# A GeGLU feed-forward kernel: the first transfers put on one queue without a gate, the first tokens turned per block of 128

## The chip, the cores and the metric

The kernel runs on one core of a Trainium2 chip. The metric is the time of one execution on the device in microseconds (us). The profile is that of one execution, taken by the hardware profiler; its times are counted from the first instruction.

## The reference

```python
B, S, D, F = 32, 32, 1024, 3584
x: (B, S, D); w_gate, w_up: (D, F); w_down: (F, D)      # all bfloat16
def reference(x, w_gate, w_up, w_down):
    return (_gelu(x @ w_gate) * (x @ w_up)) @ w_down     # gelu, tanh form
```

There are 1024 tokens. Matrix products of 1024 x 1024 x 3584 (twice) and 1024 x 3584 x 1024 are computed.

## The kernel before

**Tiling.** TensorE contracts over 128 partitions. The 1024 input features are 8 steps `dk` of 128 (feature p*8+dk sits on partition p), the 3584 hidden features are 28 chunks `m` of 128. For each chunk and each stretch of tokens the kernel accumulates a gate product ("G") and an up product ("U") in PSUM over the 8 steps, ScalarE takes the gelu of the gate into a buffer `tb`, and VectorE multiplies it by the up product into `hT`. When all of `hT` is there, the second phase multiplies it by `w_down` (line 418) and writes the result out.

**Parts.** A part is one chunk with one stretch of tokens. The first 8 chunks are done in three stretches: tokens 0 to 255 (parts 0 to 7, called XA), tokens 256 to 511 (parts 8 to 15, XB, itself of two halves XB1 and XB2 of 128 tokens), tokens 512 to 1023 (XC2). All other chunks have two stretches of 512. Parts 0 to 15 keep gate and up side by side in one PSUM bank (bank m), so that part 8 can begin only when VectorE has multiplied part 0 out of the same bank.

**x has to be turned.** Features must lie on partitions (`xT`). For XA, two blocks of 128 tokens are loaded (`xa`, line 292). TensorE turns dk 0 to 4 of them by matmuls with an identity (`turn_xa`, lines 344 to 355), ScalarE copies the result from PSUM to `xT` (line 432; the banks and steps are in `XA_PS`, line 131), and VectorE turns dk 5 to 7 (line 455). The rest of x is loaded in 512-byte rows into `xs`, which lies in a part of `hT` that is still free (line 283), and VectorE turns it (line 470).

**First weights.** The first 8 chunks need 1024 columns of both weight matrices. They are loaded step by step, wg and wu of dk 0, of dk 1 and so on, 256 KB each (`load_w0`, line 288). The text calls them wg0 to wg7 and wu0 to wu7. The later weights come in 1 MB groups (line 277), the first of which waits until XC2 has landed (`gate_w`, lines 303 to 309).

**Order of the work.** Every engine's program is written out by hand. `steps` (lines 156 to 183) is TensorE's order: turn XA; dk 0 of parts 0 to 7; dk 1 to 5 of all eight together; dk 6 and 7 of the parts 0 to 3, then of 4 to 7; then parts 8 to 11, in dk 0 to 3 first for XB1 and then for XB2; then the rest part by part. `dve_order` (lines 186 to 194) is VectorE's: "E" is the multiplication of a part, A, B, C and D are transposes of XB1, XB2, XC2 and all of XB at one dk. SyncE issues the first block of `xa`, all sixteen first weights, and then, behind a wait until wu5 has landed (line 299), one half of every x piece. ScalarE issues the second block of `xa` and, behind the same wait, the other half of every x piece. Before its first real matmul TensorE runs ten matmuls on constants (`WARM`, line 390).

The lines that decide which transfer is issued when:

```python
            ctx.set(("xa", side), ew.do(lambda: eng.dma_start(
                xa[:, side, :], xa_r[:, side, :]), clock=Q_XA[side]))
            yield
            if side == 0:
                for k in range(DK):
                    for w in ("wg", "wu"):
                        load_w0(ew, eng, w, k)
            ew.wait(Q_W0[("wu", 5)], ctx.get(("wu0", 5)))
            for q in XPIECES:
                load_x(ew, eng, q, side)
```

Of the kernel before, what the change touches and what calls it, by code (L numbers as in the profile page):

```python
# [5 lines left out]
P = 128  # L6
BF16 = mybir.dt.bfloat16
FP32 = mybir.dt.float32
ACTF = mybir.ActivationFunctionType
# [75 lines left out]
def bass_standalone__geglu_ffn__sampling_kernel(  # L85
# [13 lines left out]
    DK = D // P  # L99
# [82 lines left out]
    one_by_one(range(8, 12), 6)  # L182
# [3 lines left out]
    dve_order = []  # L186
    mix = ("E0 E1 E2 A0 E3 A1 A2 A3 B0 B1 B2 B3 E4 D4 D5 E5 D6 D7 E6 E7 "
           "C0 E8 C1 E9 C2 E10 E11 C3 C4 E12 C5 E13 C6 C7 E14 E15")
    for w in mix.split():
        if w[0] == "E":  # L190
            dve_order.append(("E", int(w[1:])))
        else:
            dve_order.append(("T", int(w[1:])) + {"A": XB1, "B": XB2, "C": XC2, "D": XB}[w[0]])
    dve_order += [("E", p) for p in range(NSHORT, NPART)]
# [25 lines left out]
    Q_X = {(q, s): _Clock(f"x{i}{s}", 16) for i, q in enumerate(XPIECES) for s in range(2)}  # L220
    Q_W0 = {(w, k): _Clock(f"{w}0k{k}", 16) for k in range(DK) for w in ("wg", "wu")}
    Q_WG = [_Clock(f"wg{j}", 16) for j in range(NG)]
# [9 lines left out]
    with ExitStack() as es:  # L232
# [54 lines left out]
        def load_w0(ew, eng, w, k):  # L287
            ctx.set((w + "0", k), ew.do(lambda: eng.dma_start(  # L288
                big[w][:, k, :], w_r[w][:, k, 0:NBIG * P]), clock=Q_W0[(w, k)]))
# [12 lines left out]

# [22 lines left out]
        def prog_sp(eng):  # L325
            sp = _Eng(ctx, eng, None)
            for _ in early_loads(sp, eng, 0):
                pass
            wd_mine = [k for k in range(len(wd_groups)) if k % 2 == 0]
# [14 lines left out]
        def turn_xa(pe, eng, b, dk):  # L344
            pe.wait(Q_XA[b], ctx.get(("xa", b)))
            j = next(j for j, (_, k0, k1) in enumerate(XA_PS) if k0 <= dk < k1)
            bank, k0, k1 = XA_PS[j]
            o = 256 * (dk - k0) + P * b
            last = dk == k1 - 1 and b == 1
            v = pe.do(lambda: eng.matmul(  # L350
                ps[:, bank, o:o + P],
                xa[:, b, :].rearrange("p (j k) -> p j k", k=DK)[:, :, dk],
                ident[:, :], start=(dk == k0 and b == 0), stop=last), mark=last)
            if last:
                ctx.set(("XP", j), v)

        def part_step(pe, eng, opened, i, key, dk, tok):
# [6 lines left out]
            if j is None:  # L364
                pe.wait(Q_W0[(w, dk)], ctx.get((w + "0", dk)))
# [4 lines left out]
            for jx, (xbank, k0, k1) in enumerate(XA_PS):  # L370
                if t0 == XA[0] and (xbank == bank or k0 <= dk < k1):
                    pe.wait(C_ACT, ctx.get(("XA", jx)))
            if t0 == XA[0] and dk >= XA_DVE[0]:
                pe.wait(C_DVE, ctx.get("XD"))
# [14 lines left out]

        WARM = [512] * 6 + [128] * 4  # L390

# [34 lines left out]
        def prog_act(eng):  # L426
            act = _Eng(ctx, eng, C_ACT)
            act.do(lambda: eng.activation(warm[:, 0:1], const0, ACTF.Gelu_apprx_tanh))
            for _ in early_loads(act, eng, 1):
                for j, (bank, k0, k1) in enumerate(XA_PS):  # L430
                    act.wait(C_PE, ctx.get(("XP", j)))
                    ctx.set(("XA", j), act.do(lambda: eng.activation(  # L432
                        xT[:, k0:k1, XA[0]:XA[1]],
                        ps[:, bank, 0:256 * (k1 - k0)].rearrange("p (k t) -> p k t", t=256), ACTF.Copy)))
            for i, (m, t0, t1, (gb, g0, g1), us) in enumerate(parts):
# [101 lines left out]
```

## Time and profile before

| what | value |
|---|---|
| median of 3 runs | 299.68 us (299.42 to 299.73) |
| profiled execution, span from first to last instruction | 298.2 us |
| the same execution's time in all | not listed beside its span |
| first phase, matmuls of line 381 on the chain | 61% of the span |
| second phase, matmuls of line 418 on the chain | 32% of the span |
| mean granted clock of TensorE | 1.000 |
| bytes moved | 26.43 MB, mean 89 GB/s |

The span leaves out what lies before the first and after the last instruction, so it is shorter than the run times. "PE" is TensorE's matmuls, "PEld" its weight loads, DVE is VectorE, ACT ScalarE, POOL GpSimd, SP SyncE; "PEq" or "SPq" is the queue of an engine that issues. The chain of waits follows the work that ended last back from the last instruction; the page gives each engine's share of it. A table of stretches gives each engine's busy time in it, with the number of instructions in brackets, the granted clock, the busy share of the DMA engines and the bytes they moved. Matmuls are pipelined: their durations overlap (a 128x256 matmul is shown with 272 ns, but eight of them start within 0.87 us), so a pace is read from starts.

### The profile page before, as it was taken

Reading aid. Unit: us, or ns where it says so; the run is one execution under the profiler, and the core shown is the slowest. Engines: PE = TensorE matmul, PEld = TensorE weight load, DVE = VectorE, ACT = ScalarE, POOL = GpSimd, SP = SyncE. Lnnn points to the kernel's source line nnn. Section 1 sums busy time; section 2 is a strip of 40 time slices with the busy share of each in tenths; the row PEclk is TensorE's granted clock in tenths of the full one; section 3 lists DMA queues with packets and bytes.
Section 4 is the critical chain, followed back from the end, with each engine's and each line's share of the span. In section 5 each row is a group of like instructions: output and inputs, shape, how many; then the busy total and the mean of one; then the engine's idle time right before and its main releaser. Section 6 shows DMA issues by size and latency. Waiting matters only on the chain.

```text
span 298.2 us, 3515 instructions
## 1 busy us (share of the span) xinstructions
PE 294.9 (99%) x1552; PEld 149.1 (50%) x1552; DVE 64.3 (22%) x108; ACT 42.2 (14%) x78; POOL 7.9 (3%) x14
## 2 busy tenths in 40 slices
PE   8999999999999999999999999999999999999997
PEld 5889644444444444444444444444444444444446
DVE  4669721111122111122111122110000000000000
ACT  3032211121111121111112111110000000000000
POOL 1001001020000002001000000000000000000000
DMA  7988004856009301943103000000000100010001
GB/s 258 391 197 263 22 2 133 289 186 240 0 0 294 131 0 31 372 162 92 51 0 141 0 2 0 0 0 20 18 18 20 35 18 18 20 35 18 18 20 35
DMA packets 17807, 26.43 MB, mean 89 GB/s; under 512 B 1025, under 2 KB 11393, under 8 KB 17793
## 3 DMA queue, kind: packets, MB, share of 16 engines
q1 hardware_dynamic: 13840, 16.78, 17.2%
q0 software_dynamic: 2176, 8.39, 7.9%
q10 hardware_dynamic: 1776, 1.05, 1.3%
q8 instruction: 12, 0.20, 0.3%
q14 instruction: 3, 0.02, 0.0%
HBM read 24.12 MB, written 2.10 MB: 88 GB/s over the span
## 4 chain that ended last, share of the span: by engine, by line
PE 94%; DMA 3%; SPq 2%; issue 0%; ACT 0%
PE ps L381 61%; PE ps L418 32%; DMA wubig<-in_w_up_dram 3%; SPq L288 2%; SPq L292 0%; ACT xT L445 0%
## 5 line engine op out<-in xcount | busy, mean ns | idle before, releaser
L418 PE MATMUL ps<-wd,hT 128*128 128x512 bf16 (+1 forms) x476 | 96.9, 366 | 0.0
L381 PE MATMUL ps<-xT,wubig 128*128 128x512 bf16 (+2 forms) x400 | 79.8, 336 | 0.3 <-DMA wubig<-in_w_up_dram 0.3
L381 PE MATMUL ps<-xT,wgbig 128*128 128x512 bf16 (+2 forms) x400 | 79.8, 336 | 0.2 <-ACT xT L432 0.2
L418 PEld LDWEIGHTS ps<-wd,hT 128*128 128x128 bf16 x476 | 46.6, 98 | 50.4
L479 DVE TENSOR_TENSOR hT<-tb,ps 128x512 bf16<-128x512 f32 (+1 forms) x64 | 39.0, 616 | 136.6 <-PE ps L381 136.6
L439 ACT ACTIVATE tb<-ps 128x512 f32<-128x512 f32 (+1 forms) x64 | 34.2, 544 | 158.4 <-PE ps L381 156.9
L381 PEld LDWEIGHTS ps<-xT,wubig 128*128 128x128 bf16 x400 | 38.1, 98 | 32.1 <-DMA wubig<-in_w_up_dram 0.7
L381 PEld LDWEIGHTS ps<-xT,wgbig 128*128 128x128 bf16 x400 | 38.0, 98 | 31.6 <-DMA wgbig<-in_w_gate_dram 0.3
L381 PE MATMUL ps<-xT,wgsmall 128*128 128x512 bf16 x128 | 30.2, 379 | 0.0
L381 PE MATMUL ps<-xT,wusmall 128*128 128x512 bf16 x128 | 30.2, 379 | 0.0
L485 DVE CAST xT<-ps 128x512 bf16<-128x512 f32 (+1 forms) x8 | 5.3, 658 | 88.1 <-PE ps L418 88.1
L381 PEld LDWEIGHTS ps<-xT,wusmall 128*128 128x128 bf16 x128 | 12.5, 98 | 15.1
L381 PEld LDWEIGHTS ps<-xT,wgsmall 128*128 128x128 bf16 x128 | 12.5, 98 | 15.1
L445 ACT ACTIVATE xT<-ps 128x512 bf16<-128x512 f32 (+1 forms) x9 | 5.2, 573 | 93.1 <-PE ps L418 93.1
L470 DVE STREAM_TRANSPOSE xT<-hT 128x128 bf16<-128x128 bf16 (+2 forms) x20 | 13.4, 714 | 0.0
L455 DVE STREAM_TRANSPOSE xT<-hT 32x192 bf16<-32x192 bf16 x16 | 8.3, 516 | 4.6 <-DMA hT<-in_x_dram 4.1
L277 POOL DMA_DIRECT2D wubig<-in_w_up_dram x3 | 2.7, 886 | 63.3 <-PE ps L381 63.3
L395 PE MATMUL ps<-const-bfloat16-1.0 128*128 128x512 bf16 (+1 forms) x10 | 3.1, 498 | 0.8 <-PEq L522 0.8
L277 POOL DMA_DIRECT2D wusmall<-in_w_up_dram x2 | 2.0, 992 | 47.3 <-PE ps L381 26.0
L271 POOL DMA_DIRECT2D wd<-in_w_down_dram x3 | 2.3, 764 | 19.1 <-PE ps L381 19.1
L395 PEld LDWEIGHTS ps<-const-bfloat16-1.0 128*128 128x128 bf16 x10 | 1.2, 139 | 2.4 <-issue 2.4
L432 ACT ACTIVATE xT<-ps 128x512 bf16<-128x512 f32 (+1 forms) x3 | 1.4, 526 | 2.2 <-PE ps L350 2.2
(10 smaller groups left out, 4.5 us busy)
## 6 DMA issues: line engine op xcount, KB each, us to landing
wd<-in_w_down_dram SPq DMA_DIRECT2D x4, 1024.0 KB, 11.5
wgbig<-in_w_gate_dram SPq DMA_DIRECT2D x3, 1024.0 KB, 5.6
wubig<-in_w_up_dram POOLq DMA_DIRECT2D x3, 1024.0 KB, 9.7
wd<-in_w_down_dram POOLq DMA_DIRECT2D x3, 1024.0 KB, 11.4
wgbig<-in_w_gate_dram SPq DMA_DIRECT2D x8, 256.0 KB, 5.5
wubig<-in_w_up_dram SPq DMA_DIRECT2D x8, 256.0 KB, 5.6
wgsmall<-in_w_gate_dram SPq DMA_DIRECT2D x2, 1024.0 KB, 5.8
wusmall<-in_w_up_dram POOLq DMA_DIRECT2D x2, 1024.0 KB, 9.7
```

The costliest lines, as they stand in the source:

```text
L271: ew.do(lambda: eng.dma_start(wd[:, a:b, :], wd_r[:, a:b, :]), clock=clock)
L277: ctx.set((w, j), ew.do(lambda: eng.dma_start(wbuf(w, buf)[:, :, 0:gsz * P], w_r[w][:, :, c0 * P:(c0 + gsz) * P]), clock=q))
L288: ctx.set((w + "0", k), ew.do(lambda: eng.dma_start(big[w][:, k, :], w_r[w][:, k, 0:NBIG * P]), clock=Q_W0[(w, k)]))
L381: v = pe.do(lambda: eng.matmul(ps[:, bank, f0:f1], wbuf(w, buf)[:, dk, slot * P:(slot + 1) * P], xT[:, dk, t0:t1], start=first, stop=last ...
L395: pe.do(lambda: eng.matmul(ps[:, 0, 0:n], ones_w, ones_x[:, 0:n], start=True, stop=True), mark=False)
L418: v = pe.do(lambda: eng.matmul(ps[:, b, 0:ncols], hT[:, m, tc * P:(tc + 1) * P], wd[:, m, col0:col0 + ncols], start=(m == 0), stop=(m == F ...
L439: ctx.set(("A", i), act.do(lambda: eng.activation(t_bufs[i % NTB][:, 0:t1 - t0], ps[:, gb, g0:g1], ACTF.Gelu_apprx_tanh)))
L445: ctx.set(("E", ji), act.do(lambda: eng.activation(osb[:, tc, col0:col0 + ncols], ps[:, b, 0:ncols], ACTF.Copy)))
L455: v = dve.do(lambda: eng.transpose(xT[32 * a:32 * (a + 1), XA_DVE[0]:XA_DVE[1], XA[0]:XA[1]].rearrange("p k (b t) -> p k b t", t=P)[:, :, ...
L470: v = dve.do(lambda: eng.transpose(xT[:, dk, q[0]:q[1]].rearrange("p (c i) -> p c i", i=32), src))
L479: ctx.set(("D", i), dve.do(lambda: eng.tensor_tensor(hT[:, m, t0:t1], t_bufs[i % NTB][:, 0:t1 - t0], ps[:, ub, u0:u1], ALU.mult)))
L485: ctx.set(("E", ji), dve.do(lambda: eng.tensor_copy(osb[:, tc, col0:col0 + ncols], ps[:, b, 0:ncols])))
```

## The change

1. SyncE issues all early transfers, and none of them waits for anything: both blocks of `xa`, the sixteen first weights, XB1 behind wu5, XB2 behind wu6 and XC2 behind wu7. ScalarE issues no transfer any more. The four quarters of an x piece go out in the order 0, 2, 1, 3.
2. The weights of dk 0 and dk 1 are loaded in halves of 512 columns (chunks 0 to 3 and 4 to 7), each with a semaphore of its own.
3. dk 0 of XA is copied from PSUM in two copies, one per block of 128 tokens (banks 7 and 6), dk 1 and 2 in one (bank 5), dk 3 and 4 in one (bank 4). TensorE does dk 0 of the gate for chunks 0, 1, 2, 3 and 7 first for block 0, then for block 1; the other products of dk 0 come in a new order.
4. Parts 8 to 11 are done with 256 tokens at once in dk 0 to 5, and VectorE turns XB only in pieces of 256 tokens (D0 to D7), D0 and D1 ahead of the first multiplication.
5. The warm-up has one matmul of 128 columns in place of four.

```diff
+    XAFTER = [(("wu", 5), (256, 384)), (("wu", 6), (384, 512)), (("wu", 7), (512, 1024))]
...
-    XA_PS = [(3, 0, 1), (4, 1, 3), (5, 3, 5)]
+    XA_PS = [(7, 0, 1, 0, 1), (6, 0, 1, 1, 2), (5, 1, 3, 0, 2), (4, 3, 5, 0, 2)]
     XA_DVE = (5, 8)
+    W0_HALVED = 2
+    w0_pieces = [(w, k, c) for k in range(8) for w in ("wg", "wu")
+                 for c in ((0, 4), (4, 8))[:2 if k < W0_HALVED else 1]]
+    w0_pieces = [(w, k, c if k < W0_HALVED else (0, NBIG)) for w, k, c in w0_pieces]
...
-    for key, ps_ in (("G", (0, 1, 2, 3, 7, 6, 4)), ("U", (0, 1, 2, 3)), ("G", (5,)), ("U", (7, 6, 4, 5))):
+    for b in range(2):
+        steps += [(p, "G", 0, (P * b, P * (b + 1))) for p in (0, 1, 2, 3, 7)]
+    for key, ps_ in (("G", (6,)), ("U", (0, 1, 2, 3)), ("G", (5,)), ("U", (7, 6, 5)), ("G", (4,)), ("U", (4,))):
         steps += [(p, key, 0, None) for p in ps_]
...
-    together(range(8, 12), 0, 4, XB1)
-    together(range(8, 12), 0, 4, XB2)
-    together(range(8, 12), 4, 6)
+    together(range(8, 12), 0, 6)
...
-    mix = ("E0 E1 E2 A0 E3 A1 A2 A3 B0 B1 B2 B3 E4 D4 D5 E5 D6 D7 E6 E7 "
+    mix = ("D0 D1 E0 E1 D2 E2 E3 D3 E4 D4 E5 D5 E6 D6 D7 E7 "
            "C0 E8 C1 E9 C2 E10 E11 C3 C4 E12 C5 E13 C6 C7 E14 E15")
...
         def load_x(ew, eng, q, side):
             c0, c1 = q[0] // 32, q[1] // 32
-            for a in (2 * side, 2 * side + 1):
+            for a in (side, 2 + side):
...
-        def early_loads(ew, eng, side):
-            ctx.set(("xa", side), ew.do(lambda: eng.dma_start(
-                xa[:, side, :], xa_r[:, side, :]), clock=Q_XA[side]))
-            yield
-            if side == 0:
-                for k in range(DK):
-                    for w in ("wg", "wu"):
-                        load_w0(ew, eng, w, k)
-            ew.wait(Q_W0[("wu", 5)], ctx.get(("wu0", 5)))
-            for q in XPIECES:
-                load_x(ew, eng, q, side)
+        def load_w0(ew, eng, pc):
+            w, k, (c0, c1) = pc
+            ctx.set(("w0", pc), ew.do(lambda: eng.dma_start(
+                big[w][:, k, c0 * P:c1 * P], w_r[w][:, k, c0 * P:c1 * P]), clock=Q_W0[pc]))
+
+        def early_loads(ew, eng):
+            for b in range(2):
+                ctx.set(("xa", b), ew.do(lambda: eng.dma_start(
+                    xa[:, b, :], xa_r[:, b, :]), clock=Q_XA[b]))
+            for pc in w0_pieces:
+                load_w0(ew, eng, pc)
+                for after, q in XAFTER:
+                    if after == pc[:2]:
+                        for side in range(2):
+                            load_x(ew, eng, q, side)
...
-        WARM = [512] * 6 + [128] * 4
+        WARM = [512] * 6 + [128]
```

More of the change, by code (lines that the diff above doesn't have):

```diff
@@ L192, in bass_standalone__geglu_ffn__sampling_kernel @@
         else:
-            dve_order.append(("T", int(w[1:])) + {"A": XB1, "B": XB2, "C": XC2, "D": XB}[w[0]])
+            dve_order.append(("T", int(w[1:])) + {"C": XC2, "D": XB}[w[0]])
     dve_order += [("E", p) for p in range(NSHORT, NPART)]
@@ L220, in bass_standalone__geglu_ffn__sampling_kernel @@
     Q_X = {(q, s): _Clock(f"x{i}{s}", 16) for i, q in enumerate(XPIECES) for s in range(2)}
-    Q_W0 = {(w, k): _Clock(f"{w}0k{k}", 16) for k in range(DK) for w in ("wg", "wu")}
+    Q_W0 = {pc: _Clock(f"{pc[0]}0k{pc[1]}c{pc[2][0]}", 16) for pc in w0_pieces}
     Q_WG = [_Clock(f"wg{j}", 16) for j in range(NG)]
@@ L285, in load_x @@
             ctx.set(("x", q, side), v)
-        def load_w0(ew, eng, w, k):
-            ctx.set((w + "0", k), ew.do(lambda: eng.dma_start(
-                big[w][:, k, :], w_r[w][:, k, 0:NBIG * P]), clock=Q_W0[(w, k)]))
-        def early_loads(ew, eng, side):
-            ctx.set(("xa", side), ew.do(lambda: eng.dma_start(
-                xa[:, side, :], xa_r[:, side, :]), clock=Q_XA[side]))
-            yield
-            if side == 0:
-                for k in range(DK):
-                    for w in ("wg", "wu"):
-                        load_w0(ew, eng, w, k)
-            ew.wait(Q_W0[("wu", 5)], ctx.get(("wu0", 5)))
-            for q in XPIECES:
-                load_x(ew, eng, q, side)
+        def load_w0(ew, eng, pc):
[12 more added lines that the diff above has]
+                            load_x(ew, eng, q, side)
         def gate_w(ew, j):
@@ L326, in prog_sp @@
             sp = _Eng(ctx, eng, None)
-            for _ in early_loads(sp, eng, 0):
-                pass
+            early_loads(sp, eng)
             wd_mine = [k for k in range(len(wd_groups)) if k % 2 == 0]
@@ L345, in turn_xa @@
             pe.wait(Q_XA[b], ctx.get(("xa", b)))
[L346 to L349, printed above, removed]
+            j, (bank, k0, k1, b0, b1) = next(
+                (j, c) for j, c in enumerate(XA_PS) if c[1] <= dk < c[2] and c[3] <= b < c[4])
+            o = P * ((b1 - b0) * (dk - k0) + b - b0)
+            last = dk == k1 - 1 and b == b1 - 1
             v = pe.do(lambda: eng.matmul(
@@ L352, in turn_xa @@
                 xa[:, b, :].rearrange("p (j k) -> p j k", k=DK)[:, :, dk],
-                ident[:, :], start=(dk == k0 and b == 0), stop=last), mark=last)
+                ident[:, :], start=(dk == k0 and b == b0), stop=last), mark=last)
             if last:
@@ L364, in part_step @@
             if j is None:
-                pe.wait(Q_W0[(w, dk)], ctx.get((w + "0", dk)))
+                pc = next(q for q in w0_pieces if q[:2] == (w, dk) and q[2][0] <= m < q[2][1])
+                pe.wait(Q_W0[pc], ctx.get(("w0", pc)))
             else:
@@ L369, in part_step @@
                 pe.wait(C_DVE, ctx.get(("D", bank_before[i][bank])))
-            for jx, (xbank, k0, k1) in enumerate(XA_PS):
-                if t0 == XA[0] and (xbank == bank or k0 <= dk < k1):
+            for jx, (xbank, k0, k1, b0, b1) in enumerate(XA_PS):
+                if t1 <= XA[1] and (xbank == bank or (k0 <= dk < k1 and t0 < P * b1 and P * b0 < t1)):
                     pe.wait(C_ACT, ctx.get(("XA", jx)))
-            if t0 == XA[0] and dk >= XA_DVE[0]:
+            if t1 <= XA[1] and dk >= XA_DVE[0]:
                 pe.wait(C_DVE, ctx.get("XD"))
@@ L428, in prog_act @@
             act.do(lambda: eng.activation(warm[:, 0:1], const0, ACTF.Gelu_apprx_tanh))
[L429 to L434, printed above, removed]
+            for j, (bank, k0, k1, b0, b1) in enumerate(XA_PS):
+                act.wait(C_PE, ctx.get(("XP", j)))
+                nt = P * (b1 - b0)
+                ctx.set(("XA", j), act.do(lambda: eng.activation(
+                    xT[:, k0:k1, P * b0:P * b1],
+                    ps[:, bank, 0:nt * (k1 - k0)].rearrange("p (k t) -> p k t", t=nt), ACTF.Copy)))
             for i, (m, t0, t1, (gb, g0, g1), us) in enumerate(parts):
```

## The prediction

> **What bounds the kernel now.** I read the page first: engines' shares, slices, chain.
>
> ```profile
> span 298.2 us, 3515 instructions
> PE 294.9 (99%) x1552; PEld 149.1 (50%) x1552; DVE 64.3 (22%) x108; ACT 42.2 (14%) x78; POOL 7.9 (3%) x14
> ...
> PE   8999999999999999999999999999999999999997
> PE 94%; DMA 3%; SPq 2%; issue 0%; ACT 0%
> ```
>
> TensorE is the bound; the only things on the chain that are not its own work lie at the start. So I read the chain of waits in order of time:
>
> ```profile
> 8.17 0.44 SPq L288
> 8.61 0.04 issue
> 8.66 8.20 DMA wubig<-in_w_up_dram
> 16.86 0.05 issue
> 16.91 182.50 PE ps L381 x951
> 199.40 96.78 PE ps L418 x476
> ```
>
> From 16.91 us on TensorE runs to the end without a stop (182.50 + 96.78 us). The last thing that held it was one transfer: the up-weights' row 7 (wu7), the last of the sixteen first pieces, issued at 8.66, landed at 16.86. The end of the kernel is "when does wu7 land" plus fixed matmul work, unless the change makes another wait later. Next, the stretches around it (columns: busy us of PE, PEld, DVE, ACT, POOL, granted clock, DMA share, GB/s):
>
> ```profile
> 4.50:5.50 1.00, 0.80 (x10) 0.63 (x9) 0.94 (x3) 1.00 (x3) 0.00 (x0) 1.00 1.03 272
> 5.50:14.00 8.50, 8.50 (x80) 7.46 (x78) 6.93 (x14) 0.26 (x1) 0.00 (x0) 1.00 1.05 392
> 14.50:16.50 2.00, 2.00 (x20) 1.66 (x18) 0.00 (x0) 0.00 (x0) 0.00 (x0) 1.00 1.09 258
> 16.50:17.50 1.00, 0.74 (x8) 0.54 (x7) 0.00 (x0) 0.28 (x1) 0.00 (x0) 1.00 0.64 145
> 17.50:19.50 2.00, 2.00 (x22) 1.80 (x20) 1.86 (x6) 1.47 (x6) 0.00 (x0) 1.00 1.06 305
> ```
>
> From 5.5 to 14 us the DMA engines are full and move weights at 392 GB/s. When the x pieces (512-byte rows) flow, the engines are just as full but move 258 to 305. Last, the queues between 14.0 and 15.6 us:
>
> ```profile
> q1 hardware_dynamic: 466, 0.36, 76.7%
> q10 hardware_dynamic: 272, 0.13, 31.6%
> q8 instruction: 1, 0.02, 4.1%
> ```
>
> q1 is SyncE's queue, q10 ScalarE's, and q8 one fetch of 16 KB of instructions (it starts at 14.45 and takes 1.05 us on one of the 16 engines). In the trace's semaphore updates fifteen engines had delivered their part of wu7 by 15.57; the sixteenth came at 16.86. The piece before it, wg7, landed at 14.76 (issued at 8.17, 6.6 us to landing).
>
> **The change, part by part.** All is measured against the span of 298.2; the page gives that execution no other time, and the median of the runs, 299.68, lies 1.48 us above it, which I add unchanged.
>
> *x pieces ahead of the last weights.* Before, x waits until wu5 is in (12.74) and then goes out on two queues beside wg6 to wu7. After, SyncE issues 4 pieces of XB1 (64 KB each) behind wu5 and 4 of XB2 behind wu6. wu7 thus has 2 x 262 KB ahead of it in its own queue. Without any x, wu7 would have landed one weight piece after wg7: wu5 to wg7 is three pieces in 14.76 - 12.73 = 2.03 us, 0.68 each, so 15.44. XB1 and XB2 at 258 GB/s take 1.02 us each, 2.03 together: 17.47. The trace has no 512-byte rows on one queue alone, so I bound it: as fast as weights (392 GB/s) 1.34 together; at the slowest full us with x in flight (145 GB/s) 3.62. I take 258, the nearest row: the same pieces at the same place. The Trainium skill, "DMA: Bandwidth & Descriptors", section "Issuing engines are not separate DMA queues", says that all queues end on the same 16 engines, so that a second queue saves only issue time; by it one queue is as fast as two and 2.03 stands, while if half the pace were lost with the second queue it would be 4.06.
>
> *Issue time.* Before, SyncE issued 16 weights from 0.73 to 8.66: (8.66 - 0.73) / 16 = 0.496 us each with gaps. After, wu7 has 29 issues ahead of it: 2 xa, 8 halves, 8 whole pieces (dk 2 to 5), 4 of XB1, wg6, wu6, 4 of XB2, wg7. 0.73 + 29 x 0.496 = 15.1 us; at 0.47 a piece, 14.4. The shortest 256 KB landing in the trace is 2.9 us after issue (xa's first block, 0.73 to 3.63), which gives 17.3 to 18.0. So the issue side reaches about the same time as the bytes; they do not add up, the later one counts. wg7 and wu7 are what stands behind the x issues on SyncE; nothing else of the first 35 us but XC2 and the small weights does.
>
> *The late engine.* The fetch belongs to TensorE's own instructions and comes at nearly the same place (3 warm-up matmuls fewer, 5 more in dk 0). It should again meet the queue before wu7 and hold one engine up. Bounds: 0 us (a gap in the queue lets that engine catch up, which an issue-bound queue gives) and 16.86 - 15.57 = 1.29 us. Between them I take 0.6: wu7 lands at 17.47 + 0.6 = 18.1.
>
> *Chunk 0 by blocks, halves, warm-up.* Three cold 128-column warm-up matmuls go (0.107 each, 0.32 us). The first copy needs only block 0, is 128 columns wide (the 128x256 copy took 0.384), and xa's second block now follows the first instead of sharing with it. Ten 128-column matmuls at 0.056 replace five at 0.109: nothing. Waits added on TensorE are for halves: behind each stands the whole matmul order. A half is issued every 0.496 us, the eight take 4.0 instead of 2.0 us, and wu1's second half leaves at about 0.73 + 9 x 0.496 = 5.2, 2.6 us later than wu1 before. With 2.0 us to landing (an estimate: 2.9 for the first 256 KB less half of its bytes' time and the ramp) it lands near 7.2, where wu1 landed before at 7.16; TensorE wants it at 7.8. I expect the first real matmul near 4.7 (before 4.93) and dk 0 done about 0.2 us earlier (between 0.0 and 0.7). TensorE would then want wu7 at 16.38 - 0.2 = 16.2. All of this lies under the wait until 18.1 and is worth nothing; were the cover gone, it would be those 0.2 us.
>
> *Transposes and parts 8 to 11.* 64 matmuls of 128 columns (19.43 to 23.00, 3.57 us) become 32 of 256 (0.1093 each, 3.50): -0.07. Eight transposes of 128x128 and four of 128x256 become eight of 128x256, 0.585 us each; D0 and D1 need XB2, which lands before wg7, and are done while TensorE waits. In TensorE's terms (part 8 starts 2.5 us after wu7) the fourth product E3 then ends about 0.08 us before it is wanted, so a stall there is 0 to 0.1; I take 0. XC2 follows wu7 and is in by about 22.5; its transposes begin near 25.5. Cover for all of them: the products E4 to E7 are wanted only 7 us after part 8's start. ScalarE loses six x issues (12.75 to 16.5), which ended before its first gelu at 17.23: nothing.
>
> Sum: TensorE resumes at 18.1 + 0.05 = 18.15 instead of 16.91, +1.24; -0.07; span 298.2 + 1.17 = 299.4, time 300.85, so **300.9 us**.
>
> **The rivals.**
> *Hidden (within 0.2%).* The queue never stops, x runs at 305 GB/s (0.86 each: 17.16) and the late engine catches up: TensorE resumes at 17.2, +0.3 - 0.07: 299.9. For it: the DMA share of 1.09 at 258 GB/s is already not the best x pace. Against: an instruction fetch in the same stretch.
> *Faster.* The gated start and two competing queues were the trouble, and one ungated queue removes it: x at 392 GB/s gives 15.44 + 1.34 = 16.78, the hole at 4.5 to 5.5 (272 instead of 392 GB/s, 0.31 us) is filled, 16.5, and without a late engine (its usual lag is 14.76 - 14.58 = 0.18) 16.3. Then TensorE's own pace counts: 16.91 less its stall of 0.43 and 0.2 of earlier start, 16.28: -0.63 - 0.07, 299.0. It decides if wu7 lands before 16.3. Against: 0.52 MB more ahead of wu7.
> *One queue is slow for x.* At 145 GB/s wu7 lands 1.59 later: 302.4. For it: the row 16.50:17.50; against: that stretch has a share of 0.64, so it lacked issues, not pace.
> *The clock falls.* The wait of 16.2 to 18.1 would send TensorE back to the pace of its first 3.4 us (128 columns in 0.107 instead of 0.056 until 4.18); 3.4 us at half rate cost 1.7: 302.6. Against: the stall of 0.43 us at 16.4 changed no matmul's time. The same loss at the start (fewer warm-up matmuls, then 0.3 us idle before xa lands) would be covered: 16.2 + 1.7 = 17.9, before 18.1. The Trainium skill, "TensorE: Matmul & The Clock Gate", section "Part 1: The HAM clock gate", asks for an idle window of about 3.4 us before the clock drops; by it a wait of 1.9 us leaves it alone, and this rival falls away.
>
> **How the numbers follow.** Forecast (300.3 to 301.6) 0.50, hidden 0.21, faster 0.10, slow queue 0.11, clock 0.08. A measurement of this kernel tells 0.2% (0.6 us) from no change: faster is below 299.1, slower above 300.3. Slower 0.50 + 0.11 + 0.08 = 0.69, less 0.01 for its lower edge: 0.68; same 0.22; faster 0.10. The range leaves the quickest tenth and part of the clock rival out: 299.4 to 302.2.
>
> **What would show it.** TensorE's longest early wait should be for wu7 (or wg7), ending near 18.1, with a rise of the start-to-resume time of 1.2 us and 279 us of matmuls behind it as before; the x pieces must have landed before wg7. The issue times on SyncE must reach 14.4 to 15.1 for wu7. If fifteen engines deliver wu7 by 17.5 and one later, the late engine is shown. I am wrong if wu7 lands before 16.3, if TensorE's waits after 20 us exceed 0.2 us, or if 256-column matmuls take longer than 0.11 us apiece after the wait.

## The result, and the profile after

| | before | after |
|---|---|---|
| median of 5 runs each | 299.68 us (299.42 to 299.84) | 307.69 us (306.03 to 308.58) |
| profiled execution, span | 298.2 us | 304.7 us |
| the same execution's time | | 306.03 us |
| mean granted clock of TensorE | 1.000 | 0.994 (two of the five runs 0.989) |

The ratio is 1.0257, with a 95% interval of 1.0230 to 1.0284: the change makes the kernel slower by 8.0 us, where 1.2 were forecast. A run more than 1.5% above the fastest of its kernel counts as slow and is left out of the ratio, which happened once below. The profiled execution is the fastest of the five; the median run took 1.66 us more at the same mean clock, and no trace shows where. The page of the kernel after, cut to the rows shown before:

```profile
span 304.7 us, 3455 instructions
PE 298.0 (98%) x1522; PEld 149.1 (49%) x1522; DVE 64.2 (21%) x104; ACT 42.6 (14%) x79; POOL 7.9 (3%) x14
...
PEclk9998999999999999999999999999999999999999
```

TensorE still is the bound, and the row of the granted clock has a dent in its fourth slice (22.9 to 30.5 us) that a glance passes over. The end of the chain of waits, in order of time:

```profile
14.65 0.43 SPq L294
15.08 0.04 issue
15.12 6.66 DMA wubig<-in_w_up_dram
21.78 0.05 issue
```

The same transfer holds TensorE as before, wu7, but it lands at 21.78 us instead of 16.86. TensorE resumes at 21.83 and then needs 304.7 - 21.83 = 282.87 us to the end, where it needed 298.2 - 16.91 = 281.29 before. So of the 6.5 us that the span grew by, 4.92 lie before the resume and 1.58 behind it. The stretches (busy us of PE, PEld, DVE, ACT, POOL; granted clock, DMA share, GB/s) show both parts:

```profile
5.50:14.00 8.50, 8.02 (x73) 6.35 (x73) 6.97 (x14) 0.30 (x1) 0.00 (x0) 1.00 0.94 319
14.50:16.50 2.00, 2.00 (x21) 1.79 (x20) 0.00 (x0) 0.00 (x0) 0.00 (x0) 1.00 1.10 278
16.50:17.50 1.00, 0.72 (x8) 0.41 (x6) 0.00 (x0) 0.00 (x0) 0.00 (x0) 1.00 1.22 287
17.50:19.50 2.00, 0.97 (x8) 0.39 (x5) 0.00 (x0) 0.00 (x0) 0.00 (x0) 1.00 1.06 286
19.50:22.00 2.50, 0.45 (x3) 0.26 (x4) 1.14 (x2) 0.00 (x0) 0.00 (x0) 1.00 1.22 210
22.40:25.80 3.40, 3.40 (x19) 2.42 (x17) 2.70 (x7) 1.61 (x6) 0.00 (x0) 0.50 0.67 125
```

From 5.5 to 14 us, where almost nothing but weights flows, the DMA engines deliver 319 GB/s instead of 392, and TensorE starts 73 matmuls instead of 80. From 16.5 to 22 it starves: 19 matmuls in 5.5 us. From 22.4 to 25.8 it is busy all the time at half its clock. The matmuls themselves, in the timeline of TensorE (start, duration, line, tiles, shape, count):

```profile
20.33 0.28 PE L386 MATMUL ps<-xT,wgbig 128*128 128x256 bf16 x1 [1.25 <-DMA wgbig<-in_w_gate_dram]
21.83 0.28 PE L386 MATMUL ps<-xT,wubig 128*128 128x256 bf16 x1 [1.22 <-DMA wubig<-in_w_up_dram]
...
23.62 1.06 PE L386 MATMUL ps<-xT,wubig 128*128 128x256 bf16 x4
...
26.02 0.60 PE L386 MATMUL ps<-xT,wgbig 128*128 128x256 bf16 x4
```

Four matmuls of 256 columns take 1.06 us at 23.6 and 0.60 at 26.0. The trace's clock records put the half rate at 22.42 to 25.83, 3.41 us, which costs half of that, 1.71.

When the pieces landed, by the semaphore updates of the trace (us). A piece has landed when the last of the 16 DMA engines has delivered its share; the mean over the 16 is beside it, since one engine alone can be more than 1 us behind:

| | wg0 | wu1 | wg2 | wu5, mean / last | XB1 | wg6 | XB2 | wg7 | wu7, mean / last | stage wu5 to wu7 by the means |
|---|---|---|---|---|---|---|---|---|---|---|
| before | 4.76 | 7.16 | 7.98 | 12.39 / 12.73 | | 13.40 | | 14.76 | 15.32 / 16.86 | 2.93 |
| after | 5.72 | 8.75 | 9.47 | 14.59 / 15.55 | 16.56 | 17.20 | 19.57 | 20.28 | 20.27 / 21.78 | 5.69 |

This splits the 4.92 us: 2.20 had already been lost when wu5 was in, before the first piece of x was due; the stage from wu5 to wu7, the only one in which x lies ahead of weights, became 2.76 longer; the last engine is as far behind the mean of wu7 as before (1.51 and 1.54). Three questions go to the chip: what makes wu5 late, what makes x cost 2.8 us, and what makes the clock fall.

### The profile page after: what moved, and what is told of

It is laid out like the page before. It is cut to its first block, busy times and chain, and to the rows that moved or that the text cites. A ratio compares the mean times of both kernels' runs of the same rounds, so it can differ in the third digit from the quotient of the medians.

```text
span 304.7 us, 3455 instructions
## 1 busy us (share of the span) xinstructions
PE 298.0 (98%) x1522; PEld 149.1 (49%) x1522; DVE 64.2 (21%) x104; ACT 42.6 (14%) x79; POOL 7.9 (3%) x14
## 4 chain that ended last, share of the span: by engine, by line
PE 92%; SPq 4%; DMA 2%; issue 0%; ACT 0%
PE ps L386 60%; PE ps L423 32%; SPq L294 3%; DMA wubig<-in_w_up_dram 2%; SPq L288 1%; SPq L299 0%; ACT xT L450 0%
## 5 line engine op out<-in xcount | busy, mean ns | idle before, releaser
L386 PE MATMUL ps<-xT,wgbig 128*128 128x512 bf16 (+2 forms) x389 | 80.9, 345 | 1.9 <-DMA wgbig<-in_w_gate_dram 1.8
L386 PE MATMUL ps<-xT,wubig 128*128 128x512 bf16 (+1 forms) x384 | 80.7, 347 | 1.9 <-DMA wubig<-in_w_up_dram 1.8
L386 PEld LDWEIGHTS ps<-xT,wusmall 128*128 128x128 bf16 x128 | 12.5, 98 | 15.1
L386 PEld LDWEIGHTS ps<-xT,wgsmall 128*128 128x128 bf16 x128 | 12.5, 98 | 15.1
L450 ACT ACTIVATE xT<-ps 128x512 bf16<-128x512 f32 (+1 forms) x9 | 5.2, 573 | 93.1 <-PE ps L423 93.1
L475 DVE STREAM_TRANSPOSE xT<-hT 128x256 bf16<-128x256 bf16 (+1 forms) x16 | 13.4, 857 | 6.8 <-DMA hT<-in_x_dram 6.8
L437 ACT ACTIVATE xT<-ps 128x128 bf16<-128x128 f32 (+1 forms) x4 | 1.6, 436 | 2.0 <-PE ps L354 2.0
```

Of the source, the lines that this page charges most:

```text
L386: v = pe.do(lambda: eng.matmul(ps[:, bank, f0:f1], wbuf(w, buf)[:, dk, slot * P:(slot + 1) * P], xT[:, dk, t0:t1], start=first, stop=last ...
L450: ctx.set(("E", ji), act.do(lambda: eng.activation(osb[:, tc, col0:col0 + ncols], ps[:, b, 0:ncols], ACTF.Copy)))
L475: v = dve.do(lambda: eng.transpose(xT[:, dk, q[0]:q[1]].rearrange("p (c i) -> p c i", i=32), src))
```

## Experiments

Each ratio is against the kernel before, timed beside it (its medians lie between 299.56 and 299.74 us). Landings are those of the profiled execution, wu5 and wu7 by the mean over the 16 engines unless the last is named; the stage is the time between these means. Expectations that give a landing or the length of a stage mean the last engine's.

### What makes wu5 late

**One part undone.** In the kernel after, the first weights in whole pieces:

```diff
-    W0_HALVED = 2
+    W0_HALVED = 0
```

> The changed kernel with the weights of dk 0 and 1 in whole pieces again (18 issues of 256 KB instead of 26); x still goes ahead of wg6 and wg7. In the changed kernel wu5 landed at 15.55 us (before: 12.73), 2.8 us late before any x had moved. Theory A (the halves starve the DMA engines: one issue each 0.47 us carries 128 KB): wu5 lands near 13.0, wu7 near 19.2 (the x stage keeps its 6.2 us from wu5 to wu7), TensorE resumes there, about 2.6 us sooner than in the changed kernel: 303.5 to 305.5 us, depending on whether the clock still falls (1.7 us). Theory B (the single ungated queue itself is slow, halves or not): wu5 stays near 15.5, the time stays at 306 to 308.6.

305.24 us (303.39 to 307.87), 1.0196 [1.0131, 1.0261]. wu5 landed at 13.35 instead of 14.59: better, but not back at 12.39. So the halves are not all of it. The trace shows the clock at half rate from 7.20 to 10.62.

**x behind all weights.** In the kernel after:

```diff
-    XAFTER = [(("wu", 5), (256, 384)), (("wu", 6), (384, 512)), (("wu", 7), (512, 1024))]
+    XAFTER = [(("wu", 7), (256, 384)), (("wu", 7), (384, 512)), (("wu", 7), (512, 1024))]
```

> The changed kernel with all x pieces issued behind wu7; the halves stay. Theory A (x ahead costs what its bytes cost, halves cost 2.8 us before it): wu5 lands near 15.5 as in the changed kernel, wu7 2.8 us later at 18.3 instead of 21.8; the clock holds, since the waits of TensorE are shorter. XB2 then lands near 20.5 and D0, D1, which VectorE does ahead of the first product, end near 21.7, so that part 8 waits about 1 us: 301 to 303 us. Theory B (the order of x does not matter, the queue is slow anyway): above 305 us.

305.15 us (304.3 to 305.61), 1.0184 [1.0162, 1.0205]: a miss. wu5 landed at 14.41, as late as in the kernel after, so x behind it is not what delays it; wu7 at 17.45, a stage of 3.04 as before the change. The gain was lost again elsewhere, as the timeline of TensorE shows (waits in brackets):

```profile
22.88 0.61 PE L386 MATMUL ps<-xT,wgbig 128*128 128x256 bf16 x2 [1.28 <-DVE hT L484]
24.05 0.72 PE L386 MATMUL ps<-xT,wgbig 128*128 128x256 bf16 x2 [0.56 <-DVE hT L484]
```

XB2 now landed at 21.26. The transposes D0 and D1 stand ahead of the first multiplications in VectorE's order, and part 8 cannot have its bank before the product E0: TensorE waits 1.28 and 0.56 us for VectorE, and the clock falls (half rate 23.87 to 27.28).

**Both together.**

> Both edits: whole pieces and x behind wu7, still one queue without a gate, everything else of the change as it is. If the two causes are independent and make up the loss: wu7 lands at 15.3 to 16.0 and TensorE has no wait over 0.5 us before 17 us; D0 and D1 are late (XB2 lands near 17.8, E0 follows at 19.2 where part 8 wants it at 18.7), 0.3 to 1 us: 299.0 to 300.5 us. If something else of the change costs (copies by block, warm-up, order of transposes), 301 us or more.

303.40 us (302.95 to 303.56), 1.0126 [1.0111, 1.0141], again above what was expected. wu5 13.17, wu7 16.11. The waits of TensorE's weight loads between 4 and 24 us (total, times, longest):

```profile
PEld ps L386 <- DMA wgbig<-in_w_gate_dram: 1.9, 1, 1.9
PEld ps L386 <- DVE hT L484: 1.5, 4, 0.8
```

The first weights landed at 6.59 instead of 4.76, although they went out in whole pieces with no x in sight. What is left of the change in these microseconds is the second block of `xa` on SyncE's queue.

**The halves alone**, put into the kernel before:

```diff
-                for k in range(DK):
-                    for w in ("wg", "wu"):
-                        load_w0(ew, eng, w, k)
+                for pc in w0_pieces:
+                    load_w0(ew, eng, pc)
```

> The kernel before with nothing but the weights of dk 0 and 1 in halves (x gated on two queues as before). If halves starve the engines: wu5 lands at about 15.0 to 15.5, x follows it by the gate, wu7 lands about 2 us later than before, near 18.5 to 19: 301.5 to 302.5 us. If the halves alone cost nothing and the slow first 11 us belong to the second block of xa on the same queue or to the x issues, 299.5 to 300 us.

300.69 us (300.55 to 301.31), 1.0045 [1.0031, 1.0060]. The stretch that had 392 GB/s and 80 matmuls before:

```profile
5.50:14.00 8.50, 7.47 (x68) 6.38 (x67) 6.97 (x14) 0.42 (x1) 0.00 (x0) 1.00 0.92 306
```

306 GB/s and 68 matmuls. wg2 landed at 10.01 (before 7.98), wu5 at 14.13, 1.74 later than before. TensorE waited 1.2 us for wg2, and then, from 10.05, ran to the end without a stop: wu7's last engine came at 17.91, but TensorE, late already, was no longer ahead of it. The halves do not lie under the wait for wu7: they move wu7 (by 1.65 us in the mean), and here they also made TensorE wait earlier.

**The second block of `xa` on SyncE alone**, put into the kernel before:

```diff
-            ctx.set(("xa", side), ew.do(lambda: eng.dma_start(
-                xa[:, side, :], xa_r[:, side, :]), clock=Q_XA[side]))
+            for b in range(2 if side == 0 else 0):
+                ctx.set(("xa", b), ew.do(lambda: eng.dma_start(
+                    xa[:, b, :], xa_r[:, b, :]), clock=Q_XA[b]))
```

> The kernel before with the second block of xa issued by SyncE behind the first instead of by ScalarE; nothing else. In the two runs with whole pieces on one queue, wg0 landed at 6.27 and 6.59 us (before: 4.76), and TensorE stood still for 2.0 us in its cold first stretch. Theory Q (the second block in front of the weights on the same queue is what makes wg0 late): wg0 lands after 5.5, TensorE's first real matmuls wait, the clock rises a window late: 300.5 to 302.5 us. Rival (the lateness has to do with what follows on the queue, or with the other edits): wg0 lands at 4.8 to 5.3 and the time is 299.4 to 300.2 us.

300.52 us (10 runs, 299.82 to 301.7), 1.0030 [1.0012, 1.0047]. The profiled execution is one of the three at 301.6 to 301.7. Its timeline:

```profile
5.74 1.67 PE L382 MATMUL ps<-xT,wgbig 128*128 128x256 bf16 x7 [0.64 <-DMA wgbig<-in_w_gate_dram]
7.21 1.06 PE L382 MATMUL ps<-xT,wubig 128*128 128x256 bf16 x4
```

The first real matmul starts at 5.74 (before 4.93) and the matmuls run at half pace until about 9.4, where before the pace doubled at 4.18. wu5 landed at 13.34, 0.95 later than before. From 5.74 on TensorE did not stop, so in this execution the loss is the late start and the half pace, and not a wait for wu7.

**The same block put back on ScalarE, in the kernel after:**

```diff
-            for b in range(2):
-                ctx.set(("xa", b), ew.do(lambda: eng.dma_start(
-                    xa[:, b, :], xa_r[:, b, :]), clock=Q_XA[b]))
+            ctx.set(("xa", 0), ew.do(lambda: eng.dma_start(
+                xa[:, 0, :], xa_r[:, 0, :]), clock=Q_XA[0]))
...
+            ctx.set(("xa", 1), act.do(lambda: eng.dma_start(
+                xa[:, 1, :], xa_r[:, 1, :]), clock=Q_XA[1]))
```

> The changed kernel with only the second block of xa given back to ScalarE's queue; halves and x ahead stay. If that block on SyncE's queue is a main cause of the slow first 11 us: wu5 lands at 13.5 to 14.5 instead of 15.55 and the time falls by 1 to 2 us, 304 to 306.5. If halves and x ahead are the causes and the block is not: wu5 near 15 to 15.5, wu7 near 21.3, 305.5 to 308.5 us.

307.27 us (305.43 to 308.1), 1.0246 [1.0209, 1.0284]: no gain that can be told from the kernel after. wu5 14.23, wu7 20.29, and the clock at half rate for two windows (21.75 to 28.58).

The landing of wu5 sorts all kernels of the study by how their first transfers go out, whatever happens to x:

| first weights | `xa` | wu5, mean of 16 engines |
|---|---|---|
| whole | two queues | 12.31 to 12.92 (before and nine others) |
| whole | one queue | 13.17, 13.34, 13.35 |
| halves | two queues | 14.13, 14.23 |
| halves | one queue | 14.41, 14.59, 14.93 (after in the middle) |

So the block on SyncE's queue costs 0.8 to 1.0 us here, the halves 1.7 to 1.8, and both 2.0 to 2.5. These are landings of wu5 against 12.39, one execution for each kernel.

### What x ahead of the last weights costs

**Whole pieces and `xa` on two queues**, so that nothing but x ahead on one queue is left of the changed transfers: the kernel above with `W0_HALVED = 0`.

> x ahead of the last weights alone: the changed kernel with whole pieces and the second block of xa on ScalarE's queue, so that the first 12 us are those of the kernel before, and XB1, XB2 on SyncE's queue behind wu5 and wu6. If the pace of 258 GB/s that the prediction took for x on one queue holds, wu5 lands at 12.7, wu7 at 12.7 + 4.76 = 17.5 plus at most 1.3 for a late engine, and the time is 300.3 to 301.5 us, the clock holds. If the stage wu5 to wu7 takes 6.0 to 6.8 us as in the five kernels that have it so far, wu7 lands at 18.7 to 19.5: 301.6 to 302.5 us, or 303.3 to 304.2 where the clock falls.

304.63 us (303.92 to 306.33), 1.0172 [1.0136, 1.0208]. wu5 12.43, as before; wu7 17.70 (last engine 19.81), a stage of 5.27. Two stretches around the wait:

```profile
16.25:19.65 3.40, 1.28 (x11) 0.75 (x8) 1.14 (x2) 0.00 (x0) 0.00 (x0) 1.00 1.19 240
19.70:23.00 3.30, 3.15 (x15) 2.26 (x16) 2.29 (x6) 1.54 (x4) 0.00 (x0) 0.50 0.70 132
```

11 matmuls in 3.4 us, and then 3.3 us at half clock. x ahead brings some 4.9 us by itself, the fall of the clock in it.

**The same with half of each x piece on ScalarE's queue**, behind waits for wu4, wu5 and wu6:

```diff
-                        for side in range(2):
-                            load_x(ew, eng, q, side)
+                        load_x(ew, eng, q, 0)
...
+            for (_, q), g in zip(XAFTER, (("wu", 4), ("wu", 5), ("wu", 6))):
+                act.wait(Q_W0[g + ((0, NBIG),)], ctx.get(("w0", g + ((0, NBIG),))))
+                load_x(act, eng, q, 1)
```

> The same, but half of each x piece (quarters 2 and 3) is issued by ScalarE when wu4, wu5 and wu6 have landed, the other half (quarters 0 and 1) by SyncE behind wu5, wu6, wu7: the same bytes ahead of wu7, on two queues. If one queue is what makes x slow, the stage wu5 to wu7 shrinks from 6.0-6.8 to about 4.8 us and the time is 1 to 1.5 us below the one-queue run. If it is the bytes and their 512-byte rows between the weights, whatever the queue, the time is the same within 0.5 us.

305.71 us (303.5 to 307.73), 1.0198 [1.0142, 1.0255]; stage 5.06. One queue is not told apart from two.

**The quarters of a piece in their natural order** (0, 1, 2, 3), on one queue:

```diff
-            for a in (side, 2 + side):
+            for a in (2 * side, 2 * side + 1):
```

> x ahead alone on one queue, with the quarters of a piece issued 0, 1, 2, 3 instead of 0, 2, 1, 3. A quarter lands on 32 partitions. If neighbouring quarters get in each other's way (the reason an alternating order would have), the stage wu5 to wu7 becomes longer by 0.3 us or more and the time rises by as much; if not, the time is the same within 0.5 us as in the other order.

305.49 us over four runs (303.47 to 308.63, of which the last is not in the ratio), 1.0170 [1.0109, 1.0232]; stage 5.19. No difference beyond the spread.

**x behind wu7**, one queue, no gate, whole pieces, `xa` on two queues, products E0 to E2 ahead of D0:

```diff
-    XAFTER = [(("wu", 5), (256, 384)), (("wu", 6), (384, 512)), (("wu", 7), (512, 1024))]
+    XAFTER = [(("wu", 7), (256, 384)), (("wu", 7), (384, 512)), (("wu", 7), (512, 1024))]
...
-    mix = ("D0 D1 E0 E1 D2 E2 E3 D3 E4 D4 E5 D5 E6 D6 D7 E7 "
+    mix = ("E0 E1 E2 D0 E3 D1 D2 D3 E4 D4 D5 E5 D6 D7 E6 E7 "
```

> One queue, no gate, whole pieces, but x behind wu7, the second block of xa on ScalarE's queue and the products E0 to E2 ahead of D0: what the change says in 'one queue, ungated' without x ahead, halves and the shared xa queue. If these three are the whole loss, it takes 299.2 to 300.2 us, no different from before by more than 0.2%. If an ungated queue costs by itself: 300.5 us or more. It can beat the kernel before only by what TensorE waits there: 0.43 us for wu7 and some 0.3 at the start.

300.11 us (10 runs, 299.17 to 300.4), 1.0011 [1.0000, 1.0021]; wu5 12.39, wu7 15.35 (last engine 16.85), stage 2.95 with no x ahead at all. This matters twice: one ungated queue costs at most 0.2%, and x behind the gate, as it was before (stage 2.93), had cost wu7 nothing. The wait has moved on, as the chain of waits shows (wu7 is no longer in it):

```profile
19.61 0.64 DVE xT L476
20.25 0.14 issue
20.39 179.89 PE ps L385 x896
```

Part 8 begins at 20.39 instead of 19.43, held by D0, the first transpose of XB, whose second half landed at 19.49.

**Bytes or shape?** To this kernel two spare loads of 256 KB into an unused buffer are added, one behind wu5 and one behind wu6, in three shapes (the change's x pieces are 512-byte rows on 32 partitions each). First 2 KB rows on 128 partitions, one transfer each:

```diff
+                if pc[:2] in (("wu", 5), ("wu", 6)):
+                    n = pc[1] - 5
+                    ew.do(lambda: eng.dma_start(
+                        spare[:, n, :], spare_r[:, 2 + n, :]), clock=Q_SP)
```

> x is last as in the run before it, and behind wu5 and wu6 stands a spare load of 256 KB each (two more blocks of x into a spare tile, read by nobody): 2 KB rows on 128 partitions, one issue each, the weights' own shape. If bytes alone count, the stage wu5 to wu7 is as long as with x there, 6.0 to 6.8 us. If the shape of x makes it long, it takes 6 pieces of 0.68 = 4.1 us, up to 5.4 with a late engine, and the time is about 1.4 us above the run with x last.

then 512-byte rows on 128 partitions, four transfers each:

```diff
+                    for a in range(4):
+                        ew.do(lambda: eng.dma_start(
+                            spare[:, n, 256 * a:256 * (a + 1)],
+                            spare_r[:, 2 + a, 0:256]), clock=Q_SP)
```

> The same spare bytes in 512-byte rows, four issues of 64 KB for each piece as x has them, but every issue lands on all 128 partitions. If the 512-byte rows make the stage long: 5.5 to 6.8 us from wu5 to wu7. If it is the 32 partitions: 4.1 to 5.4 us.

and 2 KB rows on 32 partitions, four transfers each:

```diff
+                    for a in range(4):
+                        ew.do(lambda: eng.dma_start(
+                            spare[32 * a:32 * (a + 1), n, :],
+                            spare_r[32 * a:32 * (a + 1), 2 + n, :]), clock=Q_SP)
```

> The same spare bytes in 2 KB rows, four issues of 64 KB for each piece, each on 32 partitions as x lands. If the 32 partitions at a time make the stage long: 5.5 to 6.8 us from wu5 to wu7. If it is the 512-byte rows: 4.1 to 5.4 us.

| ahead of wu6 and wu7, 512 KB in all | wu5 | wu7, mean / last | stage | median | ratio |
|---|---|---|---|---|---|
| nothing | 12.39 | 15.35 / 16.85 | 2.95 | 300.11 | 1.0011 [1.0000, 1.0021] |
| 2 KB rows, 128 partitions | 12.55 | 16.94 / 19.22 | 4.39 | 302.15 | 1.0078 [1.0059, 1.0097] |
| 512-byte rows, 128 partitions | 12.76 | 17.50 / 19.56 | 4.74 | 303.25 | 1.0120 [1.0097, 1.0143] |
| 2 KB rows, 32 partitions | 12.64 | 18.08 / 19.61 | 5.43 | 303.88 | 1.0134 [1.0117, 1.0151] |
| x itself: 512-byte rows, 32 partitions | 12.43 | 17.70 / 19.81 | 5.27 | 304.63 | 1.0172 [1.0136, 1.0208] |

In the good shape the spare loads cost 4.39 - 2.95 = 1.44 us, which is the pace of the weights (two pieces of 256 KB at 0.68 us each make 1.36): little but the bytes. Short rows add 0.35, rows on 32 partitions 1.04, and x itself, which has both, costs 2.32 (2.11 to 2.52 in the four kernels with x ahead and an early start like before's). The two kernels with four transfers per 256 KB differ by 0.69 in the stage, so by the means the number of transfers is not what makes 32 partitions dear. These are single executions. By the means the stage repeats to 0.2 us in the seven kernels without anything ahead of wu6 and wu7 (2.83 to 3.04) and to 0.4 in the four with x ahead, so the 0.35 for short rows is no larger than the spread.

By the last engine, which is the one that TensorE waits for, the five stages of the table are 4.1, 5.3, 6.3, 6.3 and 6.0 us. Each of the two shapes then costs about 1 us more than the same bytes in 2 KB rows on 128 partitions, and they cost the same: each of the two expectations finds its own long stage. The lag of one engine, which differs from execution to execution, enters there in full. So 32 partitions at a time cost more than their bytes by either count (1.04 and 1.0); whether short rows alone cost as much is not settled. The medians don't settle it either: they hold the clock's fall in most runs of the last two rows and the wait for D0 in the others.

### What makes the clock fall

**Matmuls on zeros in the gaps.** In the kernel after, up to six matmuls of 512 columns with a zero operand stand ahead of those that wait for wg6, wu6, wg7 and wu7; they add zeros to a bank in use:

```diff
+        HOLD = {(0, "G", 6): 2, (0, "U", 6): 3, (0, "G", 7): 6, (0, "U", 7): 6}
...
+                    for _ in range(HOLD.get(step[:3], 0)):
+                        pe.do(lambda: eng.matmul(ps[:, 0, 0:512], zero_w, ones_x,
+                                                 start=False, stop=False), mark=False)
```

> The changed kernel with 17 matmuls on a matrix of zeros (they add nothing to bank 0) put before part 0's steps wg6 (2), wu6 (3), wg7 (6) and wu7 (6), where TensorE waits 0.44, 0.77, 1.4 and 1.4 us in the changed kernel's trace; the transfers are untouched. Theory C (the wait itself makes the clock fall for one window of 3.41 us, which costs 1.7 us): all runs have clock 1.000 or at most the fall at the start, matmuls of 256 columns keep 0.109 us behind the wait, and the time is 1.5 to 1.9 us below the changed kernel's: 304.3 to 306.8 us, median near 306.0. Rival: the clock falls for another reason (a clock gate that does not look at this wait): the stretch at half rate stays, 306 to 308.6.

305.97 us (305.25 to 307.62), 1.0219 [1.0186, 1.0253], and the clock at 1.000 in every run. The median is 1.7 below that of the kernel after, although the fillers (the matmuls on zeros) ran 0.6 us past wu7's landing.

**The same with x ahead alone**, five matmuls before wg7 and five before wu7:

```diff
+        HOLD = {(0, "G", 7): 5, (0, "U", 7): 5}
```

> x ahead alone, with five matmuls of 512 columns on zeros (1.08 us) before part 0's wg7 and five before its wu7, where TensorE waits 1.33 and 1.32 us in that run; the transfers are the same. If the wait makes the clock fall: every run at clock 1.000, 1.5 to 2.0 us below x ahead alone's runs at 0.994 (303.9): 302.0 to 303.0 us, runs with an early fall aside. Rival: the fall does not depend on TensorE's idleness, then 303.9 to 306.3 as before.

302.97 us (302.2 to 303.25), 1.0107 [1.0090, 1.0123]; all runs at 1.000. The stretches that stand above for the kernel without fillers:

```profile
16.25:19.65 3.40, 1.99 (x13) 0.96 (x11) 1.14 (x2) 0.00 (x0) 0.00 (x0) 1.00 1.16 248
19.70:23.00 3.30, 3.17 (x26) 2.27 (x24) 1.56 (x5) 1.44 (x5) 0.00 (x0) 1.00 0.97 164
```

26 matmuls in place of 15 in the second stretch, at full clock, although wu7's last engine came later here (20.66 against 19.81). Without fillers the clock fell in all nine runs of these two kernels, with them in none of the eight: the waits are what makes it fall. What one fall costs is read from the half rate, 1.71 us. The medians are lower by nearly the same, 1.7 and 1.66, but in part by luck: two of the five runs after and two of the four with x ahead alone were at 0.989, twice the loss. Against the runs at 0.994 alone (median 306.81, and 303.92 and 303.95) the gain is 0.8 and 1.0 us, with wu7's last engine 1.17 and 0.85 later in the profiled executions with fillers.

How much of a wait it takes can be read from the clock records. In every trace here the rate changes only at the edges of windows of 3.41 us, and the half rate lasts for whole windows:

| kernel | window | TensorE idle in it | clock in the next window |
|---|---|---|---|
| after | 15.59 to 19.00 | 1.30 | full |
| after | 19.00 to 22.42 | 2.72 | half |
| x ahead alone | 16.25 to 19.66 | 2.46 | half |
| quarters in order | 16.48 to 19.89 | 2.43 | half |
| 2 KB rows on 32 partitions | 16.85 to 20.26 | 2.42 | half |
| x behind all weights | 20.45 to 23.87 | 2.21 | half |
| whole pieces | 3.79 to 7.20 | 2.10 | half |
| `xa` on two queues | 18.34 to 21.75 | 2.40 | half |
| `xa` on two queues | 21.75 to 25.16, itself at half rate | 2.10 by the same count (0.96 in which nothing ran) | half |
| x behind all weights | 3.39 to 6.80 | 1.73 | full |
| 512-byte rows, 128 partitions | 14.52 to 17.93 / 17.93 to 21.34 | 0.68 / 1.57 | full / full |

Idle time here is what lies between the end of one matmul at full pace and the start of the next. Counted in this way, also in windows at half rate, the same limit holds: eight such windows with 1.6 to 1.8 us were followed by full rate, and the one with 2.10 by a second window of half rate. In the last row the waits are spread over two windows, since an edge falls into them. No single wait in the window of the kernel after was longer than 1.39 us; two were enough.

### What the rest of the change is worth

**All edits except those of the transfers**, with x and `xa` on two queues behind wu5 as before, and E0 to E2 ahead of D0:

```diff
-    W0_HALVED = 2
+    W0_HALVED = 0
...
-    mix = ("D0 D1 E0 E1 D2 E2 E3 D3 E4 D4 E5 D5 E6 D6 D7 E7 "
+    mix = ("E0 E1 E2 D0 E3 D1 D2 D3 E4 D4 D5 E5 D6 D7 E6 E7 "
...
+            g = ("wu", 5, (0, NBIG))
+            ew.wait(Q_W0[g], ctx.get(("w0", g)))
```

> All edits but those of the transfers: chunk 0 by blocks, the new copies, the short warm-up, parts 8 to 11 with 256 tokens, D pieces; the transfers are those of before (two queues, whole pieces, x gated behind wu5), and the products E0 to E2 stand ahead of D0 again, since XB2 lands late there. If the rest is worth nothing (as predicted): first real matmul at 4.6 to 4.9, TensorE resumes behind wu7 at 16.9, 299.2 to 299.9 us. If the rest costs by itself (the short warm-up leaves TensorE idle and cold, or the new order stalls): 300.5 us or more, with the clock rising only after 7 us.

299.78 us (10 runs, 299.3 to 300.11), 1.0007 [0.9998, 1.0017]. Copies per block, the new order of dk 0, the shorter warm-up and the wider transposes are worth nothing that can be measured. This kernel equals the kernel before, and no kernel of this study was faster.

In medians the parts alone are: halves 1.1 us (300.69 against 299.56), `xa` on one queue 0.9 (300.52 against 299.65), x ahead 4.9 with its fall of the clock (304.63 against 299.74), the rest 0.1; together 7.0 of the 8.0. They need not add: each can lie under another's wait, and the medians mix runs with one and with two falls of the clock.

## Why the prediction was wrong

The sign, the piece (wu7) and the place were right, the size was not: 300.9 us was forecast, in a range up to 302.2, and 307.69 came. By the prediction's steps, against the profiled execution:

| step | forecast | measured | off by |
|---|---|---|---|
| landing of wu5 (taken from before as it was) | 0 | 14.59 - 12.39 = +2.20 | 2.20 |
| x ahead | +2.03 | 5.69 - 2.93 = +2.76 | 0.73 |
| late engine and tail without x (16.86 before) | 15.44 + 0.6 = 16.04, -0.82 | last engine behind the mean 1.51 against 1.54, -0.03 | 0.79 |
| behind the resume | -0.07 | +1.58 | 1.65 |

The four make 5.37, and the forecast span of 299.4 with them is 304.8; 304.7 was measured.

**The step that failed first** is "All of this lies under the wait until 18.1 and is worth nothing". It costed the halves and the second block on SyncE as changes that can only shift TensorE's early work, under a cover, and took the landing of wu5 from the trace of before. But they act on the queue that makes the cover: the halves alone moved wu5 by 1.74 us, the block alone by 0.95, and the wait until 18.1 was computed on a base that the same edit moved. Its estimate that wu1's second half would land near 7.2 shows the error early: it landed at 8.75. The issue times, which the step did cost, were right: wu7 was issued at 15.12, forecast 14.4 to 15.1. That the issues kept to their times said nothing of the DMA engines, which moved 319 GB/s from 5.5 to 14 us in place of 392.

**The second** is the rival with the clock, dismissed with "Against: the stall of 0.43 us at 16.4 changed no matmul's time". A stall of 0.43 us says nothing of one of several times that length. The prediction's own sign came: behind the wait the matmuls of 256 columns started 0.213 us apart, where it allowed 0.11. The price was right (1.7 forecast, 1.71 by the half rate). The Trainium skill, "TensorE: Matmul & The Clock Gate", section "Part 1: The HAM clock gate", has the clock halve after an idle window of about 3.4 us, and says that the window runs freely. The free-running edges agree with the table above, and so does the length; that the window must be idle throughout, as the prediction read it, does not: TensorE was idle for 2.1 to 2.7 us of the 3.41 in those that were followed by half rate. The measurement decides, and the right question would have been how much idle time a window may hold.

**The third** is the size of two terms. x was put at 258 GB/s, 2.03 us, from a stretch before in which x and weights were mixed; it cost 2.32 where the start was undisturbed and 2.76 in the kernel after, by the means. The value lies inside the bounds of 1.34 and 3.62, and the lower one, the pace of the weights, is nearly what rows of 2 KB on all partitions needed (1.44). The late engine was put at 0.6 us, between bounds of 0 and 1.29. Counted as there, from the fifteenth engine (21.18), it was 0.60 late; but the other engines had drawn apart too, so that from the mean it was as late as before (1.51 against 1.54), and the base of 16.04 without x was 0.8 us short: with x behind wu7 and nothing else ahead the last engine still came at 16.85. Between executions this lag differs: 1.50 with x behind wu7, 0.45 with the rest of the change alone, where an instruction fetch also fell between wu5 and wu7. Whether the fetch makes it was not tried; it can't be the only cause, since with x ahead alone one engine was already more than 1 us behind the others at wg1 (6.27 and 7.43), long before that trace's fetch at 14.59.

**What held.** The piece that holds TensorE, its issue time, and that the rest of the change is worth nothing; the last only where E0 to E2 stand ahead of D0, since in the order of the change D0 and D1 held part 8 up as soon as XB2 came late (1.28 and 0.56 us). The rival of the slow queue falls: half of x on a second queue left the stage at 5.06 against 5.27. The Trainium skill, "DMA: Bandwidth & Descriptors", section "Issuing engines are not separate DMA queues", says the same.

**What stays open.** Why halves, or a second block of `xa` on the queue, make the first 12 us slower. A sign of it is that more packets of 1 to 2 KB took over 250 ns between 2.5 and 13 us: 11 to 17 in nine of the ten kernels with whole pieces and `xa` on two queues and 25 in the tenth (half of x on ScalarE's queue), 31 to 43 in those with either edit or both. What holds these packets up was not found, and the runs do not say it. The halves also change two things at once, the number of transfers and the length of the rows (1 KB for 2 KB), which no run separates. The rows alone would explain little: a packet of 1 KB took 46 ns in the middle, one of 2 KB 84, which makes about 0.25 us for the 64 packets that each engine moves in place of 32 (an estimate from these durations), against 1.74 lost.

## What to carry to other kernels

A wait covers an edit only if the edit leaves the wait's own end alone: before calling something hidden under a transfer, follow that transfer's queue back and ask whether the edit adds transfers, splits them or changes queues ahead of it. Bytes put ahead of a critical transfer are paid in full at the pace of the queue, and in these runs cost about half as much again or more when they went to 32 partitions at a time. Add up TensorE's idle time per window of 3.4 us instead of looking for one long wait.

## What was not expected of the hardware

- Two waits of about 1.3 us within one window of 3.41 us halved TensorE's clock for the next window. Windows with 2.10 us idle or more did so, windows with 1.8 or less did not. Where the edges of the windows fall can decide: in the kernel with 512-byte rows on 128 partitions an edge split the waits into 0.68 and 1.57, and the clock stayed full. That may also be why the kernel after ran at a mean clock of 0.994 in three runs (306.0 to 307.7 us) and 0.989, twice the loss, in two (308.4 and 308.6); the runs at 0.989 left no trace to read it from. The one trace in this study at 0.989, with `xa` on two queues, shows two windows of half rate in a row.
- The granted clock does not show the first cold stretch. With `xa` on one queue the matmuls ran at half pace until about 9.4 us (four of 256 columns in 1.06 us at 7.21), while the stretch that holds them reads 1.00:

```profile
5.50:14.00 8.50, 8.26 (x60) 6.73 (x61) 6.92 (x14) 0.36 (x1) 0.00 (x0) 1.00 1.01 362
```

  60 matmuls instead of 80 tell it. Full pace began at 4.0 to 6.7 us in fifteen of the eighteen traces, and at 9.4 to 10.0 in three: `xa` on one queue, whole pieces with x last, and the kernel after with fillers. In these TensorE had waited 0.7 to 1.9 us for the first weights, still at half pace; that this wait is the reason was not tried by itself.
- 512 KB between large pieces of one queue cost 1.44 us in 2 KB rows on 128 partitions, 1.79 in 512-byte rows on 128 partitions and 2.48 in 2 KB rows on 32 partitions, by the mean of the 16 engines. By the last engine it is 1.2, 2.2 and 2.2, so which shape is the dearer is not settled. The Trainium skill, "DMA: Bandwidth & Descriptors", section "Specifications", gives 512 bytes as enough for full rate; here such rows were 0.35 us slower by the means, within the spread of such stages, and 1.1 by the last engine, both from single executions.
